# One-token decoder block on one core: 48-KB key rows, all queries at the start, the output issued by ScalarE, last values in two parts, w2 in four loads

## The chip, the cores and the metric

One core of a Trainium2 chip. The metric is the device time of one execution in microseconds (us), median over several executions. The profiles are one execution each; their times count from the first instruction of the program. Besides the profile's views I use the records of the single DMA packets in the same traces (start, duration, bytes); where a number comes from them the text says "packet records". All runs are of a program on one core. PE is TensorE (the matrix engine), PEld its weight loads, DVE VectorE, ACT ScalarE, POOL GpSimd, SP the sync engine. "Granted clock" is the share of PE's full clock that the profile shows as granted (PEclk).

## The reference

One token goes through an attention with a cache of 32,768 keys and values per head (32 heads of 192), then through a dense layer with ReLU.

```
x:[1,1,640]   k_cache, v_cache:[1,32,32768,192]   wq:[640,6144]   wo:[6144,640]   w1:[640,1536]   w2:[1536,640]   (bf16)
q = layernorm(x) @ wq
s = q . k_cache * 192**-0.5;  p = softmax(s);  o = p @ v_cache
h = x + o @ wo
out = h + relu(layernorm(h) @ w1) @ w2
```

Keys and values are 805 MB of the 825 MB that have to be read. There is nothing to reuse: each key and value is used once.

## The kernel before

A head has four loads of keys and four of values, 3 MB each: 128 partitions with 64 rows, 24 KB a partition. Each load is two chunks of 32 rows per partition. The scores of a chunk are split: VectorE takes 12 or 16 of the 32 rows (multiply, reduce), the rest goes over PE transposes, ScalarE copies from PSUM and PE products. ScalarE takes the exps. PE multiplies the exps (exponentials) with the values, 16 products a chunk ("value products").

```python
    kt = [sbuf(f"kt{i}", [P, JL * Dh], bf16, 512) for i in range(NL)]      # JL = 64, NL = 4: 24 KB a partition each
    vt = [sbuf(f"vt{i}", [P, JL * Dh], bf16, 512) for i in range(NV)]      # NV = 2
    ...
        load(wq_v, wq_view[:, :, 0:QG * Dh], "dwq", "wq", 0)               # wq for 8 heads at a time, rows of 3,072 B
        for h in range(H):
            for ld in range(NL if h < LAST else NL - 1):
                n = NL * h + ld
                load(kt[ld][:], rows(k_hd, h, P * JL * ld, JL), f"dk{ld}", "k", h, ld)
                if n >= NV:
                    hp, lp = divmod(n - NV, NL)
                    g.wait("PV", hp, 2 * lp + 1)                           # values of that chunk multiplied
                load(vt[ld % NV][:], rows(v_hd, h, P * JL * ld, JL), f"dv{ld % NV}", "v", h, ld)
        ... # last head: last quarter's keys in parts of 40, 16, 8 rows, then its values, then w1, w2 in 3 loads
        g.wait("y_row")
        load(out.rearrange("b s (c p) -> (b s c) p", p=P), y_row[:], "dout", "out")
        g.wait("out")
        g.do(lambda: nc.sync.nop())                                        # then the semaphores are cleared
    ...
    def pe_end(g):                                                         # the last head on PE
        ...
        transposes(g, h, E0)
        values(g, h, E0 - 1)
        for c in range(E0 + 1, NCM):
            transposes(g, h, c)
            scores_pe(g, h, c - 1)
            if c > E0 + 1:
                values(g, h, c - 2)
        scores_pe(g, h, NCM - 1)
        den_mm(g, h)
        values(g, h, NCM - 2)
        values(g, h, NCM - 1)
        ... # output projection, layer norm, w1 products, ReLU, w2 products
```

"PV h c" is the label of the value products of head h, chunk c; all loads are issued in order by the sync engine (SP in the profile), which waits for such labels when a buffer is to be overwritten.

The softmax here doesn't subtract the row's maximum and nothing guards it: scores larger than these inputs give would overflow.

## Time and profile before

| | before |
|---|---|
| time, median of 6 runs | 1923.86 us (1923.65 to 1924.11) |
| span of the profile | 1922.4 us |
| first / last packet of weights, keys, values | 2.1 / 1914.95 us (packet records) |
| last w2 product ends | 1918.12 us |
| output's DMA issued | 1919.08 us |
| two heads and one load of wo | 117.52 us, in every interval without a wq load (packet records) |

### The profile page before, as it was taken

The page shows a single profiled execution, that of the slowest core. Times are in us where ns is not written, and L with a number is a line of the kernel's source. Part 1 is how long each engine was busy: PE and PEld are TensorE (multiplying, and loading weights), DVE is VectorE, ACT ScalarE, POOL GpSimd, SP SyncE. Part 2 cuts the span into 40 slices and gives each one's busy share as a digit, 9 for nine tenths or more (in the row PEclk, how much of TensorE's full clock was granted, in tenths as well). Part 3 has the DMA queues.
Part 4 walks back from the last instruction along what each step waited for, and adds up shares of the span by engine and source line. Part 5 has one row for each costly group of instructions (what it writes and reads, how often), then busy time and mean ns, then how long its engine had stood idle before and what let it go on. Part 6 is the DMA issues. An engine that isn't in the chain of part 4 may idle for free.

```text
span 1922.4 us, 36522 instructions
## 1 busy us (share of the span) xinstructions
PE 1563.5 (81%) x15899; PEld 1073.1 (56%) x15899; DVE 1560.6 (81%) x734; ACT 970.7 (50%) x2031; POOL 0.7 (0%) x6
## 2 busy tenths in 40 slices
PE   5888888788888888788787888888878887888887
PEld 4555555555555555555555555555545555555555
DVE  5878888887887888787888878888778887888886
ACT  3555455454555555454454555545445454555554
POOL 0000000000000000000000000000000000000000
PEclk9898888988888898888898888888888888898888
DMA  9999999999999999999999999999999999999998
GB/s 405 430 431 432 432 434 433 433 431 432 433 431 433 434 433 432 432 432 428 435 434 433 432 432 433 433 432 432 432 433 433 432 433 433 432 433 433 433 430 342
DMA packets 44793, 825.26 MB, mean 429 GB/s; under 512 B 4580, under 2 KB 6116, under 8 KB 12132
## 3 DMA queue, kind: packets, MB, share of 16 engines
q1 hardware_dynamic: 44762, 824.99, 99.9%
q8 instruction: 12, 0.20, 0.0%
q14 instruction: 9, 0.07, 0.0%
q10 hardware_dynamic: 10, 0.00, 0.0%
HBM read 824.97 MB, written 0.00 MB: 429 GB/s over the span
## 4 chain that ended last, share of the span: by engine, by line
DMA 76%; PE 21%; SPq 2%; issue 1%; ACT 0%; POOLq 0%; DVE 0%
DMA kt<-in_A_k_cache_dram 76%; PE o_ps L324 11%; PE tp L343 10%; SPq L224 2%; PE sp L324 0%; PE attT L324 0%; ACT kT L538 0%; POOLq L306 0%; PE mm L324 0%; DVE o_pair L638 0%; ACT pB L544 0%; PE mm L527 0%; DVE y_row L713 0%; ACT h1T L600 0%; DVE oT L648 0%
## 5 line engine op out<-in xcount | busy, mean ns | idle before, releaser
L623 DVE TENSOR_TENSOR pr<-kt,qb 128x2304 f32<-128x2304 bf16 (+2 forms) x257 | 756.0, 2942 | 278.9 <-POOLq L290 261.5
L538 ACT COPY kT<-tp 128x1024 bf16<-128x1024 bf16 (+1 forms) x899 | 818.8, 992 | 319.3 <-PE tp L343 317.3
L343 PE MATMUL tp<-ident_f,kt 128*128 128x128 f32 x3459 | 569.7, 331 | 334.3 <-POOLq L306 334.3
L626 DVE TENSOR_REDUCE sc<-pr 128x12 f32<-128x2304 f32 (+2 forms) x257 | 755.3, 2939 | 8.9
L343 PEld LDWEIGHTS tp<-ident_f,kt 128*128 128x128 f32 x3459 | 496.1, 172 | 351.3 <-POOLq L306 350.1
L324 PE MATMUL o_ps<-vt,pB 128*2 128x384 bf16 x2286 | 472.5, 358 | 6.8 <-POOLq L306 6.6
L324 PE MATMUL o_ps<-vt,pA 128*2 128x384 bf16 x1778 | 331.0, 326 | 0.0
L324 PEld LDWEIGHTS o_ps<-vt,pB 128*2 128x2 bf16 x2286 | 184.5, 89 | 244.7 <-issue 88.3
L544 ACT ACTIVATE pB<-sp 128x20 bf16<-128x20 f32 (+2 forms) x258 | 47.9, 186 | 504.5 <-PE sp L324 504.5
L324 PEld LDWEIGHTS sp<-qm,kT 128*128 128x128 bf16 x6918 | 193.3, 97 | 77.9 <-issue 65.2
L324 PEld LDWEIGHTS o_ps<-vt,pA 128*2 128x2 bf16 x1778 | 150.7, 85 | 144.9 <-issue 7.9
L324 PE MATMUL sp<-qm,kT 128*128 128x2 bf16 x6918 | 212.0, 164 | 3.1 <-ACT kT L538 2.4
L553 ACT ACTIVATE pA<-sc 128x12 bf16<-128x12 f32 (+2 forms) x257 | 53.4, 208 | 106.4 <-DVEq L65 104.7
L544 ACT ACTIVATION_READ_ACCUMULATOR pB<-sp 128x1 f32 x258 | 50.2, 195 | 0.0
L553 ACT ACTIVATION_READ_ACCUMULATOR pA<-sc 128x1 f32 x257 | 48.7, 190 | 0.0
L631 DVE TENSOR_REDUCE rec<-mm 128x1 f32<-128x20 f32 x32 | 5.7, 179 | 50.3 <-PE mm L324 49.8
L324 PE MATMUL mm<-wq_s,xn_ln 128*1 (+1 forms) x160 | 18.7, 248 | 4.0 <-POOLq L306 4.0
L638 DVE TENSOR_SCALAR o_pair<-o_ps,rec 2x384 bf16<-2x384 f32 x32 | 19.4, 605 | 2.7 <-PE o_ps L324 1.7
L324 PE MATMUL attT<-oT,wo_s 128*128 128x1 bf16 x465 | 15.9, 163 | 0.3 <-DVE oT L648 0.3
L324 PEld LDWEIGHTS mm<-dsums,ones_mat 128*128 128x128 f32 x64 | 9.5, 188 | 10.7 <-issue 9.3
L324 PEld LDWEIGHTS attT<-oT,wo_s 128*128 128x128 bf16 x465 | 13.8, 96 | 0.4 <-DVE oT L648 0.4
L324 PE MATMUL mm<-ones_row,row_e 1*128 1x1 bf16 x384 | 14.0, 159 | 0.0
(71 smaller groups left out, 144.9 us busy)
## 6 DMA issues: line engine op xcount, KB each, us to landing
kt<-in_A_k_cache_dram SPq DMA_DIRECT2D x127, 3072.0 KB, 22.5
vt<-in_A_v_cache_dram SPq DMA_DIRECT2D x127, 3072.0 KB, 15.6
wq_s<-in_A_wq_dram SPq DMA_DIRECT2D x4, 1920.0 KB, 21.0
wo_s<-in_A_wo_dram SPq DMA_DIRECT2D x16, 480.0 KB, 16.3
kt<-in_A_k_cache_dram SPq DMA_DIRECT2D x1, 1920.0 KB, 20.2
kt<-in_A_v_cache_dram SPq DMA_DIRECT2D x2, 960.0 KB, 24.8
kt<-in_B_w_dram SPq DMA_DIRECT2D x1, 1920.0 KB, 18.5
wq_s<-in_B_w_dram SPq DMA_DIRECT2D x1, 960.0 KB, 20.5
```

The lines of the kernel that those rows point to most:

```text
L224: g.do(lambda: nc.sync.dma_start(out=dst, in_=src), sem, label, by=16)
L324: return lambda: pe.matmul(o, lhsT=w, rhs=r, **kw)
L343: calls.append(lambda b=b, o=o: pe.transpose(out=dst[:, b, :], in_=src[:, o:o + 2 * P].bitcast(f32), identity=ident_f[:]))
L538: g.do(lambda: act.copy(out=kT[c % 2][:, b0:b0 + nb, :], in_=src[:, 0:nb, :].bitcast(bf16)), "act_pe", ("cp", h, c, k))
L544: g.do(lambda: act.activation(out=pB[c % 4][:, 0:jp], in_=sp[:, 0:jp], func=F.Exp, scale=SCALE, accum_out=dsums[:, 2 * c + 1:2 * c + 2]), ...
L553: g.do(lambda: act.activation(out=pA[c % 4][:, 0:jd], in_=sc[c % NC][:, 0:jd], func=F.Exp, scale=SCALE, accum_out=dsums[:, 2 * c:2 * c + 1 ...
L623: g.chain(lambda: dve.tensor_tensor(out=pr[:, 0:j1 - j0, :], in0=src[:, (off + j0) * Dh:(off + j1) * Dh].rearrange("p (j d) -> p j d", d=D ...
L626: g.chain(lambda: dve.reduce_sum(out=sc[c % NC][:, j0:j1], in_=pr[:, 0:j1 - j0, :], axis=X), "dve")
L631: g.chain(lambda: dve.reduce_sum(out=rec[:, 0:1], in_=mm[:, 0:2 * NCM], axis=X), "dve")
L638: g.do(lambda: dve.tensor_scalar_mul(out=o_pair[:, :, 1, :], in0=o_ps[0:2, 0:2 * Dh].rearrange("q (i d) -> q i d", i=2), scalar1=rec[0:2, ...
```

## The change

The intent: fewer and longer DMA rows (keys 48 KB a partition, half of the values too), the query weights loaded at once with 12-KB rows so that no load of them comes between heads, keys before values in the last head so that the compute behind the last byte gets short, and an exit in which semaphores are cleared beside the output's transfer.

```diff
-    kt = [sbuf(f"kt{i}", [P, JL * Dh], bf16, 512) for i in range(NL)]
-    vt = [sbuf(f"vt{i}", [P, JL * Dh], bf16, 512) for i in range(NV)]
-    wq_s = sbuf("wq_s", [P, DT * QG * Dh], bf16, 512)
+    kt = [sbuf(f"kt{i}", [P, JK * Dh], bf16, 512) for i in range(NK)]     # JK = 128, NK = 2
+    va = sbuf("va", [P, JK * Dh], bf16, 512)
+    vb = sbuf("vb", [P, JL * Dh], bf16, 512)
+        def keys(h, ld):
+            if h > 0:
+                if ld == 0:
+                    g.wait("PV", h - 1, 4 if h == 1 else 2)
+                else:
+                    g.wait("PV", h - 1, 5)
+                g.wait("scs", h - 1, 4 * ld + 3)
+            elif ld == 1:
+                g.wait("att0")
+            load(kt[ld][:], rows(k_hd, h, P * JK * ld, JK), f"dk{ld}", "k", h, ld)
+        def vals(h, ld):
+            if ld == 1:
+                g.wait("PV", h, 1)
+            elif h > 0:
+                g.wait("PV", h - 1, 3 if ld == 0 else NC - 1)
+            ...
+        for c in range(DT):
+            load(wq_c[c], wq_view[:, c * H * Dh:(c + 1) * H * Dh], f"dwq{c}", "wq", c)
+        for h in range(LAST):
+            keys(h, 0)
+            vals(h, 0)
+            keys(h, 1)
+            for ld in ((2, 1) if h == 0 else (1, 2)):
+                vals(h, ld)
 ...  last head: all keys first (64, 64, 64, 40, 16, 8 rows), then all values, w1, w2
-    W2_CUTS = (0, FT // 2, FT - 2, FT)
+    W2_CUTS = (0, FT // 2, FT - 3, FT - 1, FT)
 ...  queries: 5 x 64 products of 96 columns of wq into o_ps, all heads, at the start
+            calls = [mmul(o_ps[0:HE, 2 * h + e:2 * h + e + 1], wq_c[c][:, h * Dh + e:(h + 1) * Dh:2],
+                          ln_t["ln1"]["xn"][:, c:c + 1], ...)
 ...  last head on PE
+        transposes(g, h, 9)
+        values(g, h, 2)
+        scores_pe(g, h, 8)
+        values(g, h, 3)
+        scores_pe(g, h, 9)
+        values(g, h, 4)
+        for c in (5, 6, 7):
+            values(g, h, c)
+        values(g, h, 9)
+        values(g, h, 8, 0)          # the half whose exps come from PE's scores
+        den_mm(g, h)
+        values(g, h, 8, 1)          # the half whose exps come from VectorE's scores
 ...  exit
-        load(out.rearrange("b s (c p) -> (b s c) p", p=P), y_row[:], "dout", "out")
-        g.wait("out")
+        g.do(lambda: act.dma_start(out=out.rearrange("b s (c p) -> (b s c) p", p=P), in_=y_row[:]), "dout", ("out",), by=16)
+    nc.clear_and_free_semaphores([n for n in nc.allocated_since(before) if n != sems["dout"].num])
+    nc.sync.wait_ge(sems["dout"], 16)
+    nc.sync.sem_inc(sems["dout"], -16)
```

## The prediction

> **What bounds the kernel now.** I read the page's slices first, to see whether one resource is full all the time.
>
> ```profile
> DMA  9999999999999999999999999999999999999998
> GB/s 405 430 431 432 432 434 433 433 431 432 433 431 433 434 433 432 432 432 428 435 434 433 432 432 433 433 432 432 432 433 433 432 433 433 432 433 433 433 430 342
> DMA packets 44793, 825.26 MB, mean 429 GB/s; under 512 B 4580, under 2 KB 6116, under 8 KB 12132
> ```
>
> DMA is full in 39 of 40 slices, at one flat rate; only the first and the last slice are lower. In a slice of 48.1 us the last one lacks 90 GB/s of 432, 10 us of transfer, and the first 27, 3 us. The rest is a stream that never stops. PE and DVE are busy 81% each. Next the waits, to see who waits for whom:
>
> ```profile
> PEld tp L343 <- POOLq L306: 350.1, 127, 6.4
> ...
> DVE pr L623 <- POOLq L290: 261.5, 102, 9.9
> ```
>
> Both are waits for keys that have not landed (GpSimd passes the landing on), so the engines wait for DMA. The sync queue waits too:
>
> ```profile
> SPq L224 <- PE o_ps L324: 1772.9, 126, 33.6
> ```
>
> It holds loads back until values have been used, yet the slices show no gap: a load is issued while two or three earlier ones are still queued (a key load lands 22.5 us after its issue, though 3 MB take 7.3 us). This wait costs nothing as long as it ends before the queue is empty. That leaves the two ends. Transfers begin at 2.2 us. The tail, as stretches and as the chain of waits:
>
> ```profile
> 1911.00:1912.00 1.00, 0.58 (x4) 0.10 (x2) 0.38 (x1) 0.00 (x0) 0.00 (x0) 1.00 1.06 394
> 1912.00:1913.00 1.00, 0.40 (x10) 0.32 (x10) 0.51 (x3) 0.00 (x0) 0.00 (x0) 1.00 0.91 335
> 1913.00:1914.00 1.00, 0.73 (x18) 0.65 (x18) 0.34 (x4) 0.00 (x0) 0.00 (x0) 1.00 0.61 225
> 1914.00:1915.00 1.00, 0.97 (x29) 0.88 (x29) 0.54 (x3) 0.15 (x1) 0.00 (x0) 1.00 0.26 95
> 1915.00:1916.00 1.00, 0.99 (x40) 0.90 (x37) 0.16 (x1) 0.15 (x1) 0.00 (x0) 1.00 0.08 16
> 1916.00:1919.00 3.00, 2.12 (x61) 1.75 (x61) 0.39 (x2) 0.27 (x1) 0.00 (x0) 0.59 0.00 0
> ```
>
> ```profile
> 1860.46 23.21 DMA kt<-in_A_k_cache_dram
> ...
> 1911.62 0.62 DVE o_pair L638
> ...
> 1914.34 1.67 PE o_ps L324 x60
> ...
> 1916.36 1.76 PE attT L324 x60
> ...
> 1918.77 0.28 DVE y_row L713
> ```
>
> The last two columns of the stretches are the DMA share and GB/s. The last packet of w2 ends at 1915.2, after engines that differ by 3 us (the share falls from 1.06 to 0.08). But the chain's last DMA piece is a key load that landed at 1883.7; from there it is compute alone, through the last head's remaining chunks, the layer norm, the w1 products and all 60 w2 products, which start at 1916.4, after all of w2 is in. So the last 35 us are compute-bound, by a little: 60 w2 products end at 1918.1, 2.9 us after the last byte. The output's DMA is issued at 1919.1, and the span ends at 1922.4.
>
> **What the Trainium skill says.** "DMA: Bandwidth & Descriptors", "Where 436 GB/s comes from", gives the fabric ceiling: 16 ports x 32 B x 850 MHz = 435.2 GB/s. The trace agrees: the flat slices stand at 432 to 434, so the kernel runs at 99.4% of it. The same page, "Why small descriptors are slow", names a fixed overhead per packet. The packet records show one: 24,576 B take 912 ns, 3,072 B 121 ns, 1,280 B 55 ns, which is a line of 36.8 ns per KB (1,000 B) plus 8 ns; neighbours overlap by some of it (the stretches' share is over 1.00). Its "Anatomy of one DMA" says that semaphore waits happen on the issuing sequencer and that DMA engines only drain their queues; that fits the sync queue's 1773 us of waits beside full DMA engines. For the 48-KB rows that are new, no page and no trace says whether one row stays one packet.
>
> **The change, part by part.**
>
> *Fewer, larger packets.* Between two loads of output weights the packet records move 432.6 GB/s, that is 24,576 B per engine in 908.9 ns. At the ceiling it would be 903.5, so a packet costs 5.4 ns beyond its bytes, completion record included (9 ns for 8 packets). The check: two heads and one load of output weights repeat every 117.52 us; 128 x 908.9 = 116.34 leaves 1.18 us for 8 packets of 3,840 B, 147 ns each, 6 over their 141 of bytes. Before, a head is 8 loads of 24-KB rows, 64 packets per engine. After: two key loads and one value load with 48-KB rows and two value loads with 24-KB rows, 5 x 8 = 40. 24 x 5.4 = 0.13 us a head, 4.0 us over 31 heads. wq: before 4 loads of 640 rows of 3,072 B, 160 packets per engine; after 5 of 128 rows of 12,288 B, 40: 120 x 5.5 = 0.7 us. The last head's two half loads of values add about 0.1 us. Sum: the stream ends **4.6 us** earlier, at 1910.6. Bytes are unchanged, and this alone is on the path.
>
> *wq first.* 7.9 MB come before the first key, 18.1 us instead of 4.5. DMA is as full as before and the bytes are only moved, so nothing is lost if the next buffers come free in time. 320 query products at about 30 ns (30 score products take 0.90 us) are 2 us for the last fifth, so the wait of the second key tile on them ends near 23 us; the first key tile and value tile keep DMA in work until 42.
>
> *Buffers.* Whether the stream stops is the main question: there are now two key tiles of 48 KB, one value tile of 48 and one of 24. I set the first key tile's landing to T. A head is 58.2 us of DMA; keys of a chunk cost DVE 5.1 us (12 rows: 2.56 + 2.55) or 6.7 (16 rows), 47.4 us a head. The tightest wait is that of the second value load on the values of chunk 1: T + 11.8 (DVE) + 0.4 (exp) + 2.8 (16 products) = T + 15; its place in the stream begins at T + 21.8, after the first values (7.3) and second keys (14.5). That is a margin of 6.7 us. The next head's first keys need values 2, which need the load landing at T + 29: T + 32 against T + 43.5. The others have 10 us or more. In the first head chunk 4's values free the next key tile near 68, due at 79. No gap expected.
>
> *The tail.* Let the stream end at E. Before, the keys of the last quarter land after the third quarter's values; now all keys land before the second value load: the last at about E - 31, w1 and w2 being 9.7 us and each quarter 7.3. DVE starts the last head at E - 60.5 and needs 47.7 us, and 1 us for the head before: done near E - 11. The last values need the last value load (E - 9.7) and then 0.8 + 1.5 us: done at E - 7.3. Before, from there (1911.6) to the start of the w1 products is 2.7 us: E - 4.6, with w1 landed at E - 5. Products 1.7, Relu 0.35: E - 2.5. The first three parts of w2 are done as they land, and behind the last one (one block in twelve) are 5 products, 0.3 us. So products end at E + 0.4 = 1911.0 instead of 1918.1: **7.1 us** earlier, of which 4.6 are the stream and 2.5 the compute that is no longer behind it. The split of chunk 8 around VectorE's last exps and the 4th load of w2 are part of those 2.5 us; alone they are some tenths.
>
> *The exit.* From the last product to the output's issue 0.96 us stay (ScalarE copies in place of VectorE, about the same). From the issue to the end it is 3.3 us: 0.4 issue, 0.8 wait for landing, and 2.1 of barriers and semaphore clearing. The clearing now runs beside the output's transfer. I take **1.0 us** of it as saved.
>
> *Against it:* the queries add 640 instructions before the loop; instruction fetches take packets (16 KB, about 0.9 us each) from single engines, and the slowest engine sets E. I allow 0.6 us. Sum: 7.1 + 1.0 - 0.6 = 7.5 us, 1923.8 - 7.5 = **1916.3 us**, 0.4%.
>
> **Rivals.** (1) A 48-KB row is cut into several packets, or its longer pitch in memory lowers the rate. Then the 4.0 us are lost: 1920. A rate loss of 1% would give 1935; for it speaks that the pitch doubles, against it that the limit seen is the fabric's ceiling, with the same rate at every row length once 5 ns per packet are taken off. (2) A buffer comes free too late once a head, because the tiles are coarser: each microsecond of gap costs 31 us. For it: loads of 14.5 us and only three and a half tiles; against it: the margin of 6.7 us. 2 us of gap would make 1985. (3) The tail stays compute-bound, since the value products wait to the end and the PE queue is in order: 2 to 3 us back, 1919. For it: the margin at the w1 products is under 1 us; against it: even then only the products of w2 that are late, 1.8 us for all, come behind E. (4) The late engines fall further behind: 1 to 2 us.
>
> **Range and chances.** Even at the ceiling 825 MB take 1896 us, and 2% would be 1885, so faster by 2% is excluded. Slower by 2% needs rival 2 at over 1.4 us a head or a rate 2.4% lower. Rivals 1 and 3 together give 1922; better clearing and a smaller spread of the engines 1913. So 1912.5 to 1920.5, and nearly all on "within 2%".
>
> **What would show it.** The slices should stay at 9 with GB/s at 433 to 434.5; a digit of 8 or a dip refutes the buffers' step. About 15,000 records fewer (384 packets and 48 completions a head, 1,920 packets of wq). Packets of 49,152 B near 1,816 ns in the records confirm the first step. In the tail the chain should pass through a w2 load and 5 products, with the w1 products ended before; if it goes back over values or scores, the tail's step is wrong. The gap from the output's issue to the span's end should be near 2.3 us.

## The result, and the profile after

The changed kernel: 1917.34 us, median of 6 runs (1917.0 to 1920.49); before 1923.86. The ratio is 0.997 (interval 0.9957 to 0.9983). Ratios are the mean time of one kernel's runs over that of the other's of the same rounds, so not quite the ratio of the medians. The gain is 6.5 us, 0.3%; the interval lies below 1. The runs now spread over 3.5 us where they had spread over 0.5.

The page of the changed kernel, slices and packets:

```profile
DMA  9999999999999999999999999999999999999998
GB/s 409 430 434 433 430 435 431 435 436 433 434 431 434 435 429 431 435 432 439 434 429 435 434 431 435 434 429 437 431 434 438 431 436 429 437 431 433 431 432 367
DMA packets 29650, 825.29 MB, mean 431 GB/s; under 512 B 3131, under 2 KB 4668, under 8 KB 8124
```

DMA is full as before, there are 15,143 records fewer, and the last slice has 367 GB/s where it had 342. (The slices now scatter between 429 and 439, so they are too coarse for the sign that the prediction named, 433 to 434.5; from 200 to 1800 us the mean is 433 GB/s, before 432.) In the packet records a row of 49,152 B is one packet of 1,815 ns (the 24,576-B ones still take 912), and two heads take 117.26 us in place of 117.52.

The chain of waits of the changed kernel at its end (start, duration, what):

```profile
1836.82 27.69 DMA kt<-in_A_k_cache_dram
...
1894.62 9.84 PE o_ps L360 x60
...
1905.57 0.62 DVE o_pair L718
...
1908.30 1.67 PE o_ps L360 x60
...
1910.31 1.78 PE attT L360 x60
...
1912.74 0.26 ACT y_row L679
```

The last DMA piece in it is again a key load, landed at 1864.5, and not a w2 load; all 60 w2 products again run in one go. The last w2 byte came at 1910.70 (packet records), so 1.37 us of compute are behind it, where it had been 3.16. And the stretches around it (the last two columns are DMA share and GB/s):

```profile
1910.00:1911.00 1.00, 0.69 (x25) 0.69 (x26) 0.00 (x0) 0.26 (x1) 0.00 (x0) 0.56 0.22 81
1911.00:1912.00 1.00, 1.00 (x41) 0.99 (x37) 0.00 (x0) 0.00 (x0) 0.00 (x0) 0.50 0.05 16
```

The 7.1 us between the two profiles by the four terms:

| term | before | after | difference |
|---|---|---|---|
| last w2 byte | 1914.95 | 1910.70 | -4.25 |
| from there to the last w2 product's end | 3.16 | 1.37 | -1.79 |
| to the output's issue | 0.97 | 0.95 | -0.02 |
| to the end of the span | 3.34 | 2.32 | -1.02 |
| span | 1922.4 | 1915.3 | -7.1 |

The profiled execution took 1917.12 us, one of the short ones; the median's 6.5 us hold some longer ones, and the experiments ask where those come from.

The start of the changed kernel has one place to look at. Its chain of waits there:

```profile
33.40 40.58 DMA va<-in_A_v_cache_dram
...
74.08 4.28 PE o_ps L360 x16
78.37 18.76 DMA kt<-in_A_k_cache_dram
```

The second head's first key load is issued at 78.37, behind the value products of chunk 4, and these had waited for the load of `va`, landed at 74.0. By the packet records the fastest DMA engine began the last load queued ahead of it (wo, 1.2 us) at 78.9. So this load comes at the last moment.

### The profile page after: what moved, and what is told of

It reads as the page before. It is cut to its first block, busy times and chain, and to the rows that moved or that the text cites. A ratio compares the mean times of both kernels' runs of the same rounds, so it can differ in the third digit from the quotient of the medians.

```text
span 1915.3 us, 36109 instructions
## 1 busy us (share of the span) xinstructions
PE 1551.1 (81%) x15899; PEld 1085.0 (57%) x15899; DVE 1561.3 (82%) x731; ACT 939.5 (49%) x2000; POOL 1.0 (0%) x6
## 4 chain that ended last, share of the span: by engine, by line
DVE 39%; DMA 38%; PE 15%; ACT 6%; issue 1%; DVEq 0%; POOLq 0%; SPq 0%
DMA kt<-in_A_k_cache_dram 36%; DVE sc L706 19%; DVE pr L703 18%; PE o_ps L360 7%; PE tp L379 6%; ACT kT L606 5%; DMA va<-in_A_v_cache_dram 2%; PE sp L360 1%; DVE o_pair L718 1%; ACT pA L621 1%; DVE oT L728 0%; DMA kt<-in_A_wq_dram 0%; DVE rec L711 0%; DVE rec L712 0%; DVE odd L724 0%
## 5 line engine op out<-in xcount | busy, mean ns | idle before, releaser
L360 PE MATMUL o_ps<-va,pB 128*2 128x384 bf16 x1152 | 222.1, 341 | 65.0 <-POOLq L342 65.0
L360 PE MATMUL o_ps<-vb,pB 128*2 128x384 bf16 x1152 | 213.1, 331 | 22.9 <-ACT pA L621 22.3
L360 PEld LDWEIGHTS o_ps<-va,pB 128*2 128x2 bf16 x1152 | 94.4, 86 | 161.5 <-POOLq L342 72.4
L360 PE MATMUL o_ps<-va,pA 128*2 128x384 bf16 x896 | 172.2, 334 | 0.0
L360 PE MATMUL o_ps<-vb,pA 128*2 128x384 bf16 x896 | 166.7, 326 | 0.0
L360 PEld LDWEIGHTS o_ps<-vb,pB 128*2 128x2 bf16 x1152 | 89.9, 84 | 122.2 <-ACT pA L621 28.2
L360 PEld LDWEIGHTS o_ps<-va,pA 128*2 128x2 bf16 x896 | 77.4, 86 | 76.1 <-issue 9.6
L360 PEld LDWEIGHTS o_ps<-vb,pA 128*2 128x2 bf16 x896 | 75.2, 84 | 70.2
L360 PE MATMUL o_ps<-xn_ln,kt 128*96 128x1 bf16 (+1 forms) x316 | 22.3, 208 | 2.7 <-DMA kt<-in_A_wq_dram 2.7
L360 PEld LDWEIGHTS o_ps<-xn_ln,kt 128*96 128x96 bf16 (+1 forms) x316 | 22.1, 174 | 2.8 <-issue 2.7
## 6 DMA issues: line engine op xcount, KB each, us to landing
kt<-in_A_k_cache_dram SPq DMA_DIRECT2D x3, 3072.0 KB, 21.3
```

The costliest lines, as they stand in the source:

```text
L360: return lambda: pe.matmul(o, lhsT=w, rhs=r, **kw)
```

## The experiments

Ten edited kernels and the changed kernel twice more ran, 5 runs each, in three series, each on a chip of its own; each series has its own runs of the kernel before (means 1924.0, 1924.2 and 1924.1 us). The series of e5, e6, e7 and e10 has no run of the changed kernel, so these are compared with the controls of the other two. The check called all of them correct, the two marked as wrong (e4, e9) too, so it does not notice 16 missing value products. First the measured terms of all of them, from one profile each. "First interval" is the time between the first packets of the first two wo loads, from the packet records, two heads: 117.52 in the kernel before.

| kernel | mean / median of runs (us) | first interval | last w2 byte | to last w2 product's end | output's issue to end | span |
|---|---|---|---|---|---|---|
| changed | 1918.1 / 1917.34 (6 runs) | 118.04 | 1910.70 | 1.37 | 2.32 | 1915.3 |
| c0_changed_again | 1918.3 / 1918.15 | 118.37 | 1911.25 | 1.33 | 2.32 | 1915.9 |
| e1_rows24 | 1922.8 / 1922.57 | 118.39 | 1915.30 | 1.67 | 2.31 | 1920.2 |
| e2_old_exit | 1920.5 / 1920.35 | 118.25 | 1911.01 | 3.18 | 3.42 | 1918.6 |
| e4_fewer_values | 1917.5 / 1917.16 | 118.53 | 1911.63 | 0.87 | 2.33 | 1915.8 |
| e5_early_keys | 1917.8 / 1917.35 | 117.46 | 1910.66 | 1.30 | 2.32 | 1915.2 |
| e6_late_keys | 1922.4 / 1922.39 | 123.47 | 1916.56 | 1.08 | 2.31 | 1920.9 |
| e7_tail_order | 1918.7 / 1918.93 | 118.54 | 1911.65 | 2.23 | 2.31 | 1917.2 |
| e10_all | 1918.1 / 1918.07 | 117.57 | 1910.28 | 1.59 | 2.32 | 1915.1 |
| c1_changed_again | 1918.8 / 1919.52 | 119.15 | 1911.95 | 2.41 | 2.32 | 1917.6 |
| e3_besides_undone | 1918.6 / 1918.59 | 118.33 | 1911.20 | 3.04 | 2.31 | 1917.5 |
| e11_all_filled | 1918.0 / 1917.96 | 117.49 | 1910.40 | 2.40 | 2.32 | 1916.1 |
| e9_before_fewer_values | 1923.3 / 1923.25 | 117.58 | 1915.33 | 1.72 | 3.36 | 1921.4 |

Runs of one kernel spread by 1 to 4 us, so differences of means under about 1 us decide nothing here. The terms of a profile do where they repeat: the exit does to 0.1 us, the interval in the middle of the run to 0.01; the tail (fifth column, "to last w2 product's end") does not.

The tail comes apart further in the profiles of those kernels that have the changed kernel's last head up to its first value products. All times are from start to start on PE (timeline), in us, with the granted clock of the stretch in brackets. The tail is the sum of the last four columns less the second.

| kernel | PE starts the last head's first 15 transposes, before the last w2 byte | these 15 transposes | to the first value product | 16 value products of chunk 2 | from there to the last w2 product's end |
|---|---|---|---|---|---|
| changed | 46.09 | 1.79 (1.00) | 20.84 | 3.86 (0.69) | 20.98 |
| c0 | 46.55 | 3.14 (0.55) | 20.98 | 2.71 (0.99) | 21.05 |
| c1 | 46.14 | 1.79 (1.00) | 20.84 | 4.62 (0.57) | 21.30 |
| e5 | 46.34 | 1.79 (1.00) | 20.82 | 4.05 (0.66) | 20.98 |
| e2 | 46.13 | 3.37 (0.51) | 20.84 | 4.13 (0.64) | 20.96 |
| e3 | 46.55 | 2.93 (0.59) | 21.20 | 4.51 (0.59) | 20.95 |
| e4 (16 products fewer) | 46.16 | 2.89 (0.60) | 21.24 | 4.52 (0.59) | 18.38 |

So in these profiles most of the tail's scatter sits in two short stretches of PE, and in both the time goes with the granted clock: the 16 products take 2.6 to 2.7 us divided by it in every row, and the 15 transposes 1.7 to 1.8. The first ten of the 16 products in c0, then in c1 (PE's timeline: start, duration, what):

```profile
1888.82 1.81 PE L360 MATMUL o_ps<-va,pB 128*2 128x384 bf16 x10
1888.44 3.36 PE L360 MATMUL o_ps<-va,pB 128*2 128x384 bf16 x10
```

Why the clock is low there in one run and not in another, no run shows.

**The control, c0.** No edit.

> The changed kernel itself, as the control of this chip. Theory: 6.5 to 6.8 us under the kernel before in most runs (1917.1), with one or two runs in six 2 to 3 us higher, since in the first head a key load is issued only just in time. Rival (the high runs are chance of the chip): the kernel before shows such runs as often.

Median 1918.15 (1917.13 to 1919.33), 5.8 us under its 1923.92. Only one run of five lies 6.5 us or more under it, so "in most runs" missed. The kernel before spread by 1.05 us in its 9 runs of this series, so the rival fell. Over all 16 runs of the changed kernel (with c1 below) the mean is 1918.4, some 5.6 us under the kernel before. The spread belongs to the changed kernel; its cause is taken up in e5, e6 and c1.

**The rows, e1.** Each 48-KB load in two of 24 KB:

```diff
-            load(kt[ld][:], rows(k_hd, h, P * JK * ld, JK), f"dk{ld}", "k", h, ld)
+            for i in range(2):
+                half = slice(i * JL * Dh, (i + 1) * JL * Dh)
+                load(kt[ld][:, half], rows(k_hd, h, P * JK * ld, JK)[:, half], ...)      # and va likewise
```

> The changed kernel, each load with 48-KB rows issued as two loads of 24-KB rows into the same tile, same waits. Theory (the stream gains by fewer packets): two heads and one load of output weights take 117.5 us again in place of 117.26, 24 packets x 5.4 ns x 31 heads = 4.0 us longer, about 1921.1. Rival (the stream's gain comes from the order of loads or from wq in long rows): 0 to 0.7 us longer.

Median 4.4 us longer than the control, mean 4.5. The steady interval of two heads is 117.52 us again, exactly that of the kernel before. The DMA view over 600 to 640 us, first of the changed kernel, then of e1:

```profile
DMA packets 466, 17.40 MB, mean 435 GB/s; under 512 B 48, under 2 KB 48, under 8 KB 48
```

```profile
DMA packets 793, 17.30 MB, mean 433 GB/s; under 512 B 89, under 2 KB 89, under 8 KB 89
```

Same buffers, same order, same waits, and the rate falls back. The theory holds: fewer packets are the stream's gain, 0.13 us a head, 4.0 us in 31 heads; the order of loads is not. e1 also has three loads more a head, each with a completion record per DMA engine, so by itself it does not say that the rows' length does it. The packet records do: from start to start a 24,576-B packet takes 908.3 ns, a 49,152-B one 1811.8, a completion record 5.9. The second 24,576 B cost 903.5 ns, so each packet costs 4.7 ns beyond its bytes, and of the 0.131 us a head 24 packets are 0.114 and three completion records 0.018. The longer rows of wq had no experiment; the same spacings (117.5 ns for 3,072 B, 457.5 for 12,288 B) make them worth 0.5 us. That the sum, 4.5, is more than the 4.25 measured fits the late load below.

**The exit, e2.** Output issued by the sync engine, wait, then clearing, as in the kernel before.

```diff
-    before = nc.snapshot_sems()
+    ctx.enter_context(nc.cleanup_on_exit())
-        g.do(lambda: act.dma_start(out=..., in_=y_row[:]), "dout", ("out",), by=16)
+        g.wait("y_row")                       # on the sync engine
+        load(out..., y_row[:], "dout", "out")
+        g.wait("out")
```

> The changed kernel with the exit of before: the output issued by the sync engine, a wait for its landing, and only then the semaphores cleared. Theory (the clearing had stood behind the output's landing): 1.0 us longer, from the output's issue to the end 3.3 us in place of 2.3. Rival (the gain there was the engine or chance): under 0.3 us.

The median is 2.2 us longer, twice what was expected; from the output's issue to the end the profile has 3.42 us in place of 2.32, 1.1 longer. The rest is in another term: the tail of this profile is 3.18 us, though its code is the changed kernel's (second table: both stretches ran at a low clock). So the exit is worth 1.1 us, shown by its own term, and the rest is the tail's scatter. The waits of the sync engine in e2 show what the clearing had stood behind (us in total, times, longest):

```profile
SPq L860 <- DMA out_dram<-y_row: 0.8, 1, 0.8
SPq L894 <- PEq L894: 0.7, 1, 0.7
SPq _compat.py:109 <- PEq _compat.py:109: 0.6, 1, 0.6
SPq L905 <- PEq L905: 0.5, 2, 0.4
```

The first is the landing of the output; of the three barriers the third line is the clearing's. In the changed kernel this view has no line of the clearing's barrier, and the wait at the end (`SPq L882`, behind the clearing) is 0.4 us in place of 0.8. The barrier's 0.6, these 0.4 and 0.08 of a shorter issue (0.28 us on ScalarE, 0.36 on the sync engine) are the 1.1. So of the rival, that the gain is the issuing engine, there are 0.08 us.

**The tail's work on PE, e4 (wrong).** 16 of 96 value products left out:

```diff
-        for c in (5, 6, 7):
+        for c in (6, 7):
```

> The changed kernel without the 16 value products of the last head's chunk 5; wrong on purpose. Theory (the tail waits for PE, which has all the value products from chunk 2 on in one queue, not for w2): the w2 products start up to 2.6 us earlier but are then held by the last w2 load at 1910.7, so they end at 1911.1 instead of 1912.1: 1.0 us shorter. Rival (the tail was already set by the last w2 load): 0.

Mean 0.8 us under the control (median 1.0), less than the runs' spread, and the tail is 0.87 us in place of c0's 1.33. Taken as a whole the tail gave 0.5 us for 2.6 us of work. By its parts (second table) the work left out is there in full: behind chunk 2 there are 18.4 us where the other profiles of that table have 21.0 to 21.3. What came back is the clock: chunk 2's products took 4.52 us at 0.59, where c0's took 2.71 at 0.99. So work on PE, and not w2's last load, sets the end, and the rival (0) falls.

**The key load at 78 us, e5 and e6.** The wait of the second head's first key load, one way and the other:

```diff
-                    g.wait("PV", h - 1, 4 if h == 1 else 2)
+                    g.wait("PV", h - 1, 1 if h == 1 else 2)      # e5
+                    g.wait("PV", h - 1, 5 if h == 1 else 2)      # e6
```

> The changed kernel; the first key load of the second head waits for the values of chunk 1 of the first head in place of chunk 4 (those come after the last transposes that read the tile). It is then issued near 61 us in place of 78. Theory (that load comes just too late, and DMA engines run dry at 80 to 85 us): the first two-head interval falls from 118.0 to 118.5 to about 117.3, 0.7 to 1.2 us shorter in time, and the spread of runs gets smaller. Rival (nothing runs dry there; the first interval is long because the order of loads differs in the first head): no change.

> The changed kernel; the same load waits for the values of chunk 5, so it is issued near 83.4 us in place of 78.4. Theory (no slack is left at this place): 4 to 5 us longer, near 1922, and 4 to 5 us more in the first interval. Rival (several us of slack, as the other waits have): under 1 us.

e5: issued at 62.0, and the first interval is 117.46 in place of 118.04 to 119.15 in three profiles of the changed kernel; that holds. The last byte came at 1910.66, against 1910.70, 1911.25 and 1911.95. By the bytes that all 16 DMA engines moved from 78 to 95 us (packet records) these three fell 0.4, 0.7 and 1.0 us behind e5; the interval is that of the engine that comes first. The mean is 0.3 to 1.0 us under those of the changed kernel's three series, which with this spread of runs does not decide. That the spread of runs gets smaller fell: 1916.75 to 1919.64. e6: issued at 84.5, first interval 123.47, 4.1 us longer than the control c0 of the other series by mean. Two of its stretches (DMA share and GB/s in the last two columns) show the empty queue:

```profile
82.00:83.00 1.00, 1.00 (x8) 0.50 (x6) 1.00 (x1) 1.00 (x2) 0.00 (x0) 1.00 0.00 0
83.00:84.00 1.00, 1.00 (x9) 0.52 (x7) 0.96 (x2) 0.79 (x1) 0.00 (x0) 1.00 0.00 0
```

No other wait gave the delay back: the load came 6.1 us later than in the changed kernel's profile, and the last byte 5.9 us later. So there is no slack at this place, and the changed kernel loses 0.6 to 1.7 us here, measured on the first interval against e5's, or 0.4 to 1.0 by the bytes of all engines.

**The tail's order, e7.** Second quarter's values loaded before the last two key parts; value products of chunks 2 and 3 before the last transposes:

```diff
+            if i == 0:                                             # after the part of 40 key rows
+                g.wait("PV", LAST - 1, NC - 1)
+                end_values(1, 0, JL * Dh, "dva", "v", LAST, 1)
         scores_pe(g, h, 6)
+        values(g, h, 2)
         transposes(g, h, 8)
         scores_pe(g, h, 7)
+        values(g, h, 3)
         transposes(g, h, 9)
-        values(g, h, 2)
         scores_pe(g, h, 8)
-        values(g, h, 3)
         scores_pe(g, h, 9)
```

> The changed kernel; in the last head the second quarter's values are loaded before the last two key parts, and PE takes chunks 2 and 3's value products before the last two transposes. Theory (the tail is compute, in PE's queue of value products after that load's landing): value products begin about 2.7 us earlier, the w2 products end 0.7 to 1.0 us earlier, at the last w2 load's end + 0.4. Rival (the tail is ScalarE's copies and the throttled clock, which this does not touch): 0 to 0.3 us.

The theory fell in this form. The mean is 0.4 us over c0's, within the spread. The value products began 26.7 us before the last byte in place of 23.5 and 22.4, as meant, but the tail is 2.23 us. Starting earlier does not end earlier: two groups of transposes and of scores (2.4 us of PE) now stand behind the start, PE then idled 1.26 us for ScalarE before the last scores, and the first 16 value products took 4.35 us at a granted clock of 0.61. The bound is PE's whole work since the keys landed, with ScalarE in between, and not the place of one load.

**The same with the idle time filled, e10 and e11.** e10 is e5, e7 and query products with 128 columns; e11 also moves chunk 4's value products between the last two score groups.

```diff
-            calls = [mmul(o_ps[0:HE, 2 * h + e:2 * h + e + 1], wq_c[c][:, h * Dh + e:(h + 1) * Dh:2],
+            calls = [mmul(o_ps[0:(P if h < H - 1 else HE), 2 * h + e:2 * h + e + 1],
+                          wq_c[c][:, h * Dh + e:h * Dh + (2 * P if h < H - 1 else Dh):2],
```

```diff
         scores_pe(g, h, 8)
+        values(g, h, 4)
         scores_pe(g, h, 9)
-        values(g, h, 4)
```

> The two last together (early key load, tail's order) and the query products with 128 columns of weights where they had 96. Theory: 1.4 to 2 us under the changed kernel, about 1916, the runs closer together; the 310 query products take 30 ns each in place of 82, so the second key tile of the first head is issued near 24 us in place of 33, which by itself brings nothing. Rival (query products are slow because of instruction fetch, not of the 96 columns): they stay at 80 ns.

> The kernel of e10 with chunk 4's value products between the two last score groups, where PE had stood idle 1.26 us for ScalarE. Theory: the value products end 1.2 us earlier, the w2 products end 0.4 to 0.6 us after the last w2 load (e10: 1.6), time 1.0 us under e10's and 1.5 us under the control's of this call. Rival (the throttled clock of PE takes it back, as in e7): no gain over e10 beyond 0.3 us.

The query products, changed kernel first, then e10 (timeline: start, duration, what, idle before):

```profile
7.24 20.61 PE L360 MATMUL o_ps<-xn_ln,kt 128*96 128x1 bf16 x256 [2.67 <-DMA kt<-in_A_wq_dram]
```

```profile
7.30 1.96 PE L361 MATMUL o_ps<-xn_ln,kt 128*128 128x1 bf16 x64 [2.73 <-DMA kt<-in_A_wq_dram]
```

256 in 20.6 us are 81 ns each; 64 in 1.96 us are 31. The rival (instruction fetch) falls, for e10 has as many instructions. The second key tile was then issued at 25.1 in place of 33.0, which brought nothing by itself, as expected: from 20 to 60 us both kernels moved the same bytes (packet records).

In time e10's mean is 0.3 us under c0's and e11's 0.8 under c1's, both less than the runs' spread, so the expected 1.4 to 2 and 1.5 us did not come; the runs lie a little closer together (1.7 and 1.6 us). The tail did not get shorter: 1.59 and 2.40 us. In e11 PE's idle 1.26 us has become 0.64, and behind chunk 2 it takes 23.98 us where e10 takes 24.23, a gain of 0.25 and not of 1.2. At its first value products it met this (PE's timeline, e11; then the same products of the changed kernel):

```profile
1883.61 3.36 PE L361 MATMUL o_ps<-va,pB 128*2 128x384 bf16 x10 [0.31 <-POOLq L343]
1886.77 2.12 PE L361 MATMUL o_ps<-va,pA 128*2 128x384 bf16 x6
```

```profile
1887.23 2.96 PE L360 MATMUL o_ps<-va,pB 128*2 128x384 bf16 x10
1890.03 1.14 PE L360 MATMUL o_ps<-va,pA 128*2 128x384 bf16 x6
...
1894.56 1.79 PE L360 MATMUL o_ps<-va,pB 128*2 128x384 bf16 x10
```

Ten products take 1.79 us at the full clock, and 2.96 or 3.36 where the granted clock is low; six take 1.14 or 2.12. The granted clock (third column from the end) over 1884 to 1888 is 0.50 in e11:

```profile
1884.00:1888.00 4.00, 4.00 (x14) 1.52 (x13) 3.96 (x2) 1.06 (x4) 0.00 (x0) 0.50 1.03 438
```

Chunk 2 took 5.21 us, where e10 (clock 0.65) had 4.08. So the rival named for e11 describes most of what happened, and no version beats the changed kernel beyond doubt.

**The two extras undone, e3.**

```diff
-    W2_CUTS = (0, FT // 2, FT - 3, FT - 1, FT)
+    W2_CUTS = (0, FT // 2, FT - 2, FT)
-        values(g, h, 8, 0)
         den_mm(g, h)
-        values(g, h, 8, 1)
+        values(g, h, 8)
```

> The changed kernel with the two extras undone: chunk 8's value products in one part behind the denominators, and w2 in three loads. Theory (the tail's products are one queue on PE: the last VectorE exp is done at 1901.3 and PE comes to chunk 8 at 1903.0; all 60 w2 products run in one go behind the last load): 0 to 0.2 us longer, not to be told from the control. Rival (the prediction, where products follow each w2 load as it lands): 0.3 to 0.6 us longer.

Mean 1918.6 beside c1's 1918.8 and c0's 1918.3: no difference that these runs could show. In the changed kernel's profile the last VectorE exp's accumulation ends at 1901.3 while PE comes to chunk 8 at 1903.0, so the split has nothing to hide there, and w2's parts are never waited for singly. Theory held. Its profile has a tail of 3.04 us, but not by the edit, which stands behind chunk 2: from there it took 20.95 us, the other profiles 20.96 to 21.30 (second table).

**The tail of the kernel before, e9 (wrong).** 16 value products left out:

```diff
         transposes(g, h, E0)
-        values(g, h, E0 - 1)
```

> The kernel before without the 16 value products of the last head's chunk 5; wrong on purpose. Theory (its tail is PE work behind the last keys, 2.9 us longer than the stream): 2 to 2.7 us shorter than the kernel before, near 1921.5, the w2 products ending close to the last w2 load's end + 0.4. Rival (the tail is bound by w2's transfer or by VectorE's scores): under 0.5 us.

Mean 0.8 us shorter; the tail is 1.72 us in place of 3.16. Both claims miss: the tail is work on PE, but taking 2.6 us of it away gives 1.4 us of the term, since PE then runs into ScalarE: the two groups of 9 transposes, now one behind the other, take 2.9 us with a wait for ScalarE's copies where they had taken 2.2, and before one score group PE waits 0.92 us for ScalarE's exps, where it had waited 0.77. It is a chain in which PE and ScalarE alternate, not one full queue.

**The second control, c1.** No edit.

> The changed kernel as the control of this call: 1917 to 1918.2 by the median, single runs up to 1920.5.

Median 1919.52 (1916.55 to 1919.82), above the range given. Its profile, a run of 1919.5 us, shows both sources of the longer runs at once: first interval 119.15 (1.1 us over the first profile's) and a tail of 2.41 (1.0 over). Between 75 and 80 us PE's granted clock was 0.51, where the first profile has 0.78:

```profile
75.00:80.00 5.00, 5.00 (x40) 2.22 (x39) 4.82 (x3) 0.00 (x0) 0.00 (x0) 0.51 0.96 409
```

so the value products before the key load ran slower, and it was issued at 79.35 in place of 78.37. But c0's was issued at 79.34, at a clock of 0.52, and its first interval is 118.37; so the issue explains part of c1's 119.15, and the rest of it stays open. In the tail the clock was 0.50 from 1884 to 1892, where the first profile has 0.50 and 0.79; chunk 2's products took 0.76 of the 1.0 us more (second table). The mean clock of the whole tail hides this: over the last 50 to 16 us before the last byte it is 0.85 in c0, c1 and e2 alike, with tails of 1.33, 2.41 and 3.18; it matters which instructions it falls on. That a low clock stretches these products is shown. What lowers it in one run and not in another stays open, and so does why the kernel before does not scatter so.

## Why the prediction was right, and where it was not

The time, 1917.3 against 1916.3 predicted, lies in the range, and the gain of 6.5 us is made of the three terms named; only the stream's and the exit's have the size given. By its steps:

- *Fewer, larger packets: right.* 0.13 us a head predicted, 0.13 measured (117.52 to 117.26 for two); 1,816 ns a packet predicted, 1,815 measured; rival 1 (a row cut up, a lower rate) did not happen. e1 gives it back. The prediction read the last w2 packet at 1915.2; the packet records have 1914.95. The last byte came 4.25 us earlier, 4.6 predicted; in the three kernels without the late load (e5, e10, e11: 1910.66, 1910.28, 1910.40) it came 4.3 to 4.7 earlier.
- *wq first: right in effect, wrong in a number.* Query products were taken at 30 ns, from score products that load 128 columns; with 96 columns they took 81, so the next key load came at 33 and not 23. It had 9 us left, so it cost nothing.
- *Buffers: wrong at one place.* "In the first head chunk 4's values free the next key tile near 68, due at 79." It was 78.4 to 79.4. The step forgot that chunk 4's values themselves have to land (74.0) before PE can multiply them (4.3 us). No gap was expected; there is one, of 0.6 to 1.7 us on the first interval against e5. The tightest wait of the steady part was put at T + 15 and measured at T + 16.3 (1052.7 after a landing at 1036.4), with no gap; the first DMA engine came to that load at 1055.6, T + 19.2 and not T + 21.8 (packet records). That is 2.9 us after the issue; in e6, with an empty queue, the first packet began 1.0 us after the issue (84.50 and 85.47), so about 2 us were to spare and not 6.7. Rival 2 (a gap in every head) did not happen. (Its price has a slip: 2 us in each of 31 heads on 1916 make 1978, not 1985.)
- *The tail: wrong.* Products were to end 0.4 us behind the last byte; they ended 1.3 to 2.4 us behind it in the three profiles of the changed kernel, 3.2 in e2. The step let PE do each chunk's values as they land. In fact PE is behind since the keys' landing and has the values of chunk 4 on as one block of work from 1894.6 to 1904.5; before that it meets stretches of a clock near half. The values, put at E - 7.3, were done at 1905.54, E - 5.2, and all 60 w2 products ran behind the last load (1.78 us), not 5. By the prediction's own sign (the chain goes back over values and scores, not over a w2 load) the step is refuted. Of 2.5 us expected, 1.8 came in the first profile, fewer in others. No run puts the old order of the last head back, so this gain is read from the profiles alone and is not shown by an experiment. This is rival 3, which the prediction priced at 2 to 3 us; it took 0.9 to 2.0, in e2 2.8. (A slip in it: E - 60.5 with 48.7 us of DVE is E - 11.8, not E - 11; it changes nothing.)
- *The extras: right that they are small;* in fact nothing was seen of them (e3).
- *The exit: right.* 1.0 us predicted, 1.02 and 1.1 measured.
- *The allowance of 0.6 us for late DMA engines* has no counterpart in the terms; it happened to stand for part of the two misses above. That is luck: without it the forecast would have been 1915.7, still in the range.

## What to carry to other kernels

When the DMA engines are full from the first to the last microsecond, only the number of packets, the bytes, and the two ends are left; here 24 packets fewer per engine and head were worth 4.0 us, more than all the reordering. Check each buffer's wait in the first and the last round by itself, following what the released work itself waits for: the steady rounds had about 2 us to spare, the first none. And where a tail is a chain of two engines at a varying clock, cut it into stretches from start to start and set the granted clock beside each: e4's 2.6 us of work were lost in the time and in the whole tail, and plain in the stretch they were taken from.

## What the Trainium skill lacked or had wrong

- "DMA: Bandwidth & Descriptors", "Why small descriptors are slow", gives a fixed overhead of about 3 cycles per packet and works it out for 256 B only. The runs show that it counts at 24 KB too: 8 ns a packet in the records, 4.7 from start to start, with the completion records 4.0 us of this kernel (e1). No page says outright that a 48-KB row is one packet in the records (the nearest, "Why a DMA increments its semaphore by 16 and not by 1", has cut rows only above 64 KiB, which the prediction overlooked); it is, of 1,815 ns.
- The same page, "Where 436 GB/s comes from", says that for transfers from HBM to SBUF the HBM side (about 358 GB/s) binds. With one core at work the runs show 432 (before) and 433 GB/s (after) from 200 to 1800 us, and 24,576 B more in a packet cost 903.5 ns, which for 16 engines is the fabric's 435.2 GB/s. The measurement decides, for one core with nothing beside it; the same page's table of measured sizes, also for a single core, has 425 GB/s at 16 MB.
- "TensorE: Matmul & The Clock Gate", "Weight-path perf modes", says that the fast weight load is on when the number of weights is 128. The runs agree: 81 ns a product with 96 columns, 31 with 128. Nothing was wrong here; the prediction had not looked it up.
- No page warns that a late load in one round costs its delay in full where the queue is always full; e6 shows 5.9 us of 6.1.
